# One step list for a whole attention and gated-MLP kernel in place of two, with new tables of PSUM banks and 2 KB buffers

## The chip, the cores and the metric

The kernel runs on one core of a Trainium2 chip. The time is that of the whole launch on the device, in microseconds (us); the figure for the kernel before is the median of three runs. A profile of one further execution gives, for every instruction, when it started, how long it took and which semaphore ended the wait before it. Engine names are those of the profile: PE (TensorE, matmuls), PEld (its weight loads), DVE (VectorE), ACT (ScalarE), POOL (GpSimd) and SP (SyncE, which issues every DMA here).

## What is computed

The reference, cut to what matters:

```
q, k, v: (8 batches, 8 heads, 576 tokens, 64)
k_p, v_p = mean of k, v over groups of 8 tokens            # 72 pooled tokens
attn     = softmax(q @ k_p.T / 8)                          # 576 x 72 a head
x        = (attn @ v_p), heads side by side                # (4608 tokens, 512)
xn       = x / sqrt(mean(x*x) + 1e-6) * rms_g
g, val   = xn @ w_gate, xn @ w_val                         # 512 -> 1536
out      = (silu(g) * val) @ w_out                         # 1536 -> 512
```

## The kernel before, in words

Every large product is made of three matmuls on numbers split into a high and a low part (high by high, low by high, high by low), each 128x128 by 128x512.

- **Attention** goes by batch b (0 to 7) and pair of heads p (0 to 3). The scores of a pair are the step `sc` (20 small matmuls into two PSUM tiles `pss`, line 441); then come maximum, exponential and normalisation on DVE, ACT and POOL. For batches 0 and 1 the probabilities are turned by TensorE (step `ft`, tiles `pst`, line 501). For batches 2 to 7 DVE turns them, they go to HBM and come back (steps `dw` and `dm`, tensors `turn`, `pt`). The product with the pooled v is the step `av`, one for each half u of the tokens (tile `psx`, line 523).
- **The MLP** goes by blocks i of 512 tokens (0 to 8) and chunks f of 128 hidden columns (0 to b, in base 36). Blocks 0 to 2 run 12 matmuls for the gate (`mg`) and 12 for the value (`me`, both line 1027). Blocks 3 and 4, 5 and 6, 7 and 8 run as pairs with seven products of block halves (Strassen's scheme): the steps `pr` (line 829, six matmuls, tiles `px` and `py`). Each `pr` reads its weights from HBM into one of **eight ring buffers** (tile `wp`, step `rl`, line 816): load m can be issued only when the product that used load m-8 is done. The second product is `mo` or its half `mp` (line 1079, tile `po`), and for the last pair `dp` (line 964), whose loads `dr` share the eight buffers.
- **The weights** arrive as float64 in 26 pieces and are taken apart in the first stage by ACT and DVE (steps `ca`, `cb`, `cc`, `cd`, `ch`, `cl`; the last one writes the low part, line 331).

The order of the work is written out: `ORDER` for the first stage, `LATER` for the rest, each a list of step names, and nothing is rescheduled. Every engine runs the steps that are its own in the order of the list, and waits for semaphores. PSUM has eight banks. In `ORDER` the digits behind a colon name the bank of each new PSUM tile, elsewhere the call does (as `BANK1`, `BANK2` and `DBANK`). Small 2 KB buffers have fixed roles: one for `act`, one for `hl`, two for `hh`, two named by the table `OUTS`.

Of the kernel before, what the change touches and what calls it, by code (L numbers as in the profile page):

```python
# [31 lines left out]

# [14 lines left out]

# [44 lines left out]
LATER = """  # L92
lk22 wt0 sc20:01 mg10 mx200 sb200 me10 gt10 mx201 ex200 lk21 lq21 kt1 sm200 mg11 vl10 wf00 wh01 nm200 hi10 lo10 wl01
wf01 ws01 sb201 ex201 me11 pk21 pk22 wf02 gt11 sm201 wd0 nm201 wh02 sc21:01 lk23 lv21 vl11 tr20 hi11 wh03 wl03 mo10
lq22 mx210 sb210 wl02 wf03 dw20 lo11 mx211 ex210 ws02 mg12 ws03 sm210 nm210 pk23 pv21 sb211 me12 ex211 wh04 gt12 sm211
dm20 sc22:01 lk30 nm211 tr21 dw21 wl04 mo11 wt1 mx220 sb220 vl12 ex220 hi12 ws04 lq23 av200:0 mx221 sm220 nm220 lo12
mg13 xc200 wf10 sb221 pk30 ex221 sm221 nm221 wh11 wl11 av201:1 lv22 ws11 gt13 dm21 me13 wf11 tr22 dw22 wf12 xc201 xd20
sq20 wh12 wl12 sc23:01 vl13 wf13 ws12 hi13 mo12 mx230 wh13 lq30 mx231 sb230 ex230 wl13 lo13 ws13 sm230 av210:0 dm22
pv22 nm230 mg14 xc210 wh14 sb231 lk31 wl14 ex231 sm231 wt2 av211:1 xd21 gt14 me14 lv23 nm231 wf20 pk31 xc211 sq21 jn21
av220:0 vl14 wd1 ws14 hi14 wh21 wl21 ws21 av221:1 mo13 xc220 pv23 xd22 tr23 xc221 lv30 dw23 wf21 wh23 lo14 mg15 wl23  # L100
sq22 ws23 jn22 sc30:01 pv30 lk32 gt15 me15 mx300 lq31 mx301 dm23 vl15 sb300 wf22 wh22 ex300 wl22 mo14 wf23 wh24 ws22
hi15 lo15 sm300 nm300 sb301 wl24 wt3 mg16 wd2 ws24 pk32 av230:0 me16 xc230 ex301 gt16 wf30 wh31 wl31 wf31 av231:1
xc231 xd23 sq23 jn23 lv31 wd3 ws31 mg17 mo15 vl16 hi16 sm301 lo16 sh2 wf32 wh32 wl32 gt17 ws32 sl2 rm21:1 rm20:0 rt20
wh33 nm301 tr30 wf33 wd4 pv31 dw30 me17 rc20 wl33 rt21 rc21 wh34 wl34 sc31:01 lq32 ws33 lk33 wt4 mo16 dm30 ws34 rs20
mg18 wf40 vl17 rs21 wh41 hi17 me18 wl41 ws41 wf41 mx310 sb310 ex310 lo17 wf42 mx311 wd5 gt18 sm310 av300:0 pk33 mo17
nm310 sb311 wh42 wh43 wl42 ws42 vl18 xc300 hi18 wl43 lo18 ws43 av301:1 lv32 xd30 ex311 mg19 sm311 nm311 tr31 xc301
sq30 wf43 wh44 wd6 wl44 sc32:01 mx320 lq33 ws44 gt19 me19 sb320 dw31 lk40 mx321 ex320 sm320 wt5 wf50 nm320 wh51 mg1a
mo18 vl19 hi19 sb321 ex321 lo19 wl51 ws51 wf51 sm321 wh53 pv32 wl53 nm321 tr32 wf52 wh52 sc33:01 mx330 pk40 dm31 dw32
me1a gt1a vl1a mx331 sb330 wl52 ex330 lq40 lk41 dm32 ws53 ws52 mo19 sm330 hi1a lo1a av310:0 mg1b nm330 sb331 ex331
xc310 sm331 nm331 wf53 pk41 av311:1 tr33 gt1b me1b lv33 xd31 dw33 xh20 xh21 xh22 xl21 xl20 av320:0 xh23 xl23 xl22 mo1a  # L110
xc311 xc320 kt2 wh54 wl54 wt6 wd7 vl1b hi1b pv33 lo1b ws54 sc40:01 dm33 mx400 lq41 sq31 jn31 sb400 mx401 ex400 mo1b
ev11 wf60 lk42 st11 mg20 sm400 nm400 ev10 sb401 ex401 sm401 st10 av321:1 gt20 nm401 av330:0 xd32 lv40 me20 xc321 pk42
xc330 ev12 sq32 jn32 st12 av331:1 xc331 wh61 vl20 mg21 wd8 hi20 wl61 ws61 xd33 lo20 wf61 lv41 pv40 sq33 jn33 ev13 st13
tr40 me21 gt21 wf62 sh3 dw40 sl3 rm30:0 rt30 vl21 rm31:1 mo20 hi21 rt31 lo21 wh63 wh62 wl62 wf63 ws62 sc41:01 lk43
mg22 mx410 lq42 sb410 wl63 ws63 pv41 mx411 ex410 dm40 wh64 me22 sm410 nm410 gt22 pk43 wl64 sb411 ex411 wt7 rc31 ws64
sc42:01 lk50 vl22 mo21 wf70 sm411 hi22 lo22 nm411 lq43 wd9 wh71 wl71 tr41 mg23 wf71 ws71 mx420 sb420 dw41 wf72 wh73
wl73 mx421 ex420 sm420 ws73 av400:0 me23 xc400 gt23 nm420 sb421 rs31 wh72 ex421 av401:1 xd40 wl72 wf73 vl23 hi23 mo22
lv42 sm421 dm41 xc401 ws72 lo23 wh74 nm421 rc30 sc43:01 mx431 wl74 ws74 wt8 mg24 lq50 mx430 pv42 wf80 tr42 dw42 me24
gt24 rs30 sb430 ex430 av410:0 mo23 dm42 wda vl24 sq40 sm430 hi24 xc410 yh30 lo24 nm430 mg25 yh31 yl30 wh81 sb431 yl31
ex431 av411:1 wl81 ws81 wf81 gt25 sm431 me25 wf82 lv43 pk50 nm431 wh82 xd41 xc411 sq41 jn41 av420:0 xc420 vl25 wdb  # L120
av421:1 hi25 mo24 tr43 lk51 xc421 wh83 wl83 wl82 ws82 lo25 dw43 wf83 xd42 pv43 mg26 ws83 sq42 jn42 lv50 me26 pk51 gt26
wh84 wl84 ws84 wt9 mo25 vl26 dm43 hi26 lo26 wf90 pv50 mg27 wh91 wl91 wf91 ws91 wf92 gt27 wh93 av430:0 wl93 av431:1
lv51 xc430 ws93 me27 xc431 xd43 sq43 wh92 jn43 mo26 wl92 ws92 sh4 vl27 sl4 rm41:1 wf93 hi27 wh94 lo27 wl94 pv51 rm40:0
ws94 mg28 rt40 rt41 rc40 me28 gt28 rs40 rc41 wta wfa0 wha1 wla1 mo27 wfa1 wsa1 wfa2 wha3 vl28 rs41 hi28 wla3 yh32 mg29
wsa3 lo28 wha2 wla2 ys33 me29 gt29 wsa2 yh33 wfa3 wha4 wla4 wtb mo28 ys34 yh34 wsa4 yl33 vl29 hi29 lo29 yl34 ys36 ys35
wfb0 whb1 wlb1 wfb1 yl32 wsb1 me2a mg2a gt2a whb3 yh35 wfb2 whb2 mo29 yh36 vl2a hi2a wlb2 wfb3 wsb2 wlb3 wsb3 lo2a
yl35 mg2b gt2b yl36 whb4 wlb4 me2b rl300 mo2a rl301 wsb4 vl2b hi2b lo2b mo2b rl302 rl303 rl304 rl305 ev20 st20 ev21
st21 pr300 cp30 pr301 u230 pr302 rl306 rl310 sa30 ev23 st23 kt4 ev22 st22 pr303 u330 pr304 c230 rl311 pr305 rl312 sw30
rl313 pr310 v230 rl314 vb30 pr306 v130 cp31 rl315 sc50:01 lk52 va30 pr311 rl316 lq51 hi30 mx501 lo30 pr312 u231 rl320
mx500 sb500 sa31 pk52 ex500 rl321 rl322 pr313 rl323 pr314 u331 rl324 pr315 c231 v231 rl325 sw31 mp300 mp301 rl326 vb31  # L130
# [102 lines left out]
def body(ctx: ExitStack, tc: tile.TileContext, qT, kT, vN, w1, w2, gain, out):  # L233
# [959 lines left out]
```

## Time and profile before

| | |
|---|---|
| median of 3 runs | 981.77 us (981.32 to 983.97) |
| profiled execution, first to last instruction (span) | 980.6 us |
| outside the span (median less span) | 1.2 us |
| PE busy | 963.3 us, 98% |
| DVE, ACT, POOL busy | 695.5, 488.6, 291.6 us |
| moved by DMA | 189.39 MB, mean 193 GB/s |

Busy time is the union of an engine's instructions. The ends of matmuls are modelled, so a busy PE need not be PE at its peak: what a stretch costs is better read from the starts.

### The profile page before, as it was taken

How to read it: one execution, taken by the hardware profiler on the slowest of the kernel's cores; microseconds unless marked ns; L12 is line 12 of the kernel's file. 1: busy time of each engine (PE TensorE's matmuls, PEld its weight loads, DVE VectorE, ACT ScalarE, POOL GpSimd, SP SyncE). 2: the span in 40 equal slices, each digit the busy share in tenths (PEclk: the TensorE clock that was granted, in tenths of full speed). 3: DMA queues.
4: the chain of work that ended last, by engine and by line, in shares of the span. 5: the costliest groups of instructions: out<-in, count | busy, mean ns of one | idle time of the engine just before them, and what ended most of it. 6: DMA issues, size and time to landing. Idle time of an engine off the chain costs nothing.

```text
span 980.6 us, 14131 instructions
## 1 busy us (share of the span) xinstructions
PE 963.3 (98%) x4784; PEld 758.1 (77%) x4784; DVE 695.5 (71%) x1139; ACT 488.6 (50%) x904; POOL 291.6 (30%) x285
## 2 busy tenths in 40 slices
PE   8999989999999999999999999999999999999998
PEld 7677768777777778787777778777888787888886
DVE  7999986866777858557777788876544745545565
ACT  6975765654665644347465554764223422223232
POOL 2200121666646576101111022355341001113230
PEclk9999999999999999999999999999999999999999
DMA  9436512787788751758786661877676506666665
GB/s 313 163 141 242 205 36 72 217 248 241 242 234 245 206 167 54 255 180 232 215 234 195 202 180 53 261 226 223 201 226 214 203 32 214 194 192 193 195 191 185
DMA packets 130199, 189.39 MB, mean 193 GB/s; under 512 B 10896, under 2 KB 76944, under 8 KB 128848
## 3 DMA queue, kind: packets, MB, share of 16 engines
q1 hardware_dynamic: 130128, 188.49, 62.6%
q8 instruction: 38, 0.62, 0.3%
q14 instruction: 33, 0.27, 0.1%
HBM read 132.22 MB, written 56.23 MB: 192 GB/s over the span
## 4 chain that ended last, share of the span: by engine, by line
PE 82%; DVE 6%; ACT 4%; DMA 3%; issue 2%; POOL 1%; SPq 1%; DVEq 0%; ACTq 0%; POOLq 0%
PE po L1079 20%; PE py L829 18%; PE psg L1027 17%; PE px L829 14%; PE pd L964 6%; PE pss L441 3%; PE psx L523 3%; DMA wp<-blocks 1%; DVE hl L1065 1%; ACT main L419 1%; POOL wt L751 1%; DMA turn<-sq 1%; DMA wx<-w 1%; DVE wt L313 1%; DVE mx L407 1%
## 5 line engine op out<-in xcount | busy, mean ns | idle before, releaser
L829 PE MATMUL py<-xp,wp 128*128 128x512 f32 x864 | 221.6, 392 | 1.4 <-DVE u L1149 0.8
L829 PEld LDWEIGHTS py<-xp,wp 128*128 128x128 f32 x864 | 160.8, 188 | 39.6 <-DVE u L1150 1.7
L1027 PE MATMUL psg<-xh,w 128*128 128x512 f32 x576 | 183.3, 400 | 2.1 <-DVE w L331 1.2
L1079 PE MATMUL po<-w,hh 128*128 128x512 f32 x672 | 174.3, 390 | 0.0
L829 PE MATMUL px<-xp,wp 128*128 128x512 f32 x648 | 166.9, 393 | 0.4 <-DMA wp<-blocks 0.3
L1079 PEld LDWEIGHTS po<-w,hh 128*128 128x128 f32 x672 | 126.1, 188 | 27.1 <-issue 0.4
L829 PEld LDWEIGHTS px<-xp,wp 128*128 128x128 f32 x648 | 120.1, 188 | 30.9 <-issue 2.7
L1027 PEld LDWEIGHTS psg<-xh,w 128*128 128x128 f32 x576 | 106.0, 189 | 33.7 <-issue 7.0
L1027 PE MATMUL psg<-xl,w 128*128 128x512 f32 x288 | 112.8, 393 | 0.0
L472 POOL TENSOR_TENSOR prob<-prob,sm 128x360 f32<-128x360 f32 x48 | 42.2, 880 | 228.1 <-DVE sm L468 164.1
L1079 PE MATMUL po<-w,hl 128*128 128x512 f32 x336 | 97.5, 399 | 1.6 <-DVE hl L1065 1.5
L1079 PEld LDWEIGHTS po<-w,hl 128*128 128x128 f32 x336 | 61.2, 188 | 20.0 <-DVE hl L1065 3.8
L1065 DVE TENSOR_TENSOR hl<-act,hh 128x512 fp32r<-128x512 f32 x60 | 50.0, 833 | 23.7 <-ACT hh L1057 20.2
L1143 ACT COPY hb<-px 128x512 f32<-128x512 f32 x36 | 21.1, 587 | 87.1 <-PE px L829 87.1
L1027 PEld LDWEIGHTS psg<-xl,w 128*128 128x128 f32 x288 | 54.4, 189 | 12.2 <-DVE xl L1016 0.4
L1148 ACT ACTIVATE hb<-hb 128x512 f32<-128x512 f32 x36 | 22.7, 632 | 80.8 <-DVE hb L1147 80.7
L1146 DVE TENSOR_TENSOR u<-u,py 128x512 f32<-128x512 f32 x36 | 24.6, 684 | 52.6 <-PE py L829 52.6
L964 PE MATMUL pd<-dp,wq 128*128 128x512 f32 x252 | 61.0, 389 | 0.0
L1057 ACT CAST hh<-act 128x512 fp32r<-128x512 f32 x60 | 37.2, 619 | 46.6 <-DVE act L1151 25.4
L964 PEld LDWEIGHTS pd<-dp,wq 128*128 128x128 f32 x252 | 47.3, 188 | 9.9
L751 POOL TENSOR_TENSOR wt<-wsum,wt 128x256 fp32r<-128x256 f32 x48 | 41.3, 865 | 38.6 <-ACT wt L747 38.5
L1150 DVE TENSOR_TENSOR u<-u,py 128x512 f32<-128x512 f32 x36 | 24.6, 683 | 32.5 <-PE py L829 32.4
(165 smaller groups left out, 1506.7 us busy)
## 6 DMA issues: line engine op xcount, KB each, us to landing
wp<-sum SPq DMA_DIRECT2D x144, 256.0 KB
wp<-blocks SPq DMA_DIRECT2D x108, 256.0 KB
sum<-wt SPq DMA_DIRECT2D x48, 256.0 KB
blocks<-w SPq DMA_DIRECT2D x24, 512.0 KB
wx<-w SPq DMA_DIRECT2D x10, 1024.0 KB
v<-vN SPq DMA_DIRECT2D x32, 288.0 KB
wx<-w SPq DMA_DIRECT2D x16, 512.0 KB
k<-kT SPq DMA_DIRECT2D x28, 288.0 KB
```

The lines of the kernel that those rows point to most:

```text
L441: nc.tensor.matmul(s["ps", h][:, t * SP:(t + 1) * SP], s["q"][r, o:o + P], s["pk"][r, :], start=True, stop=True)
L472: nc.gpsimd.tensor_tensor(l_pr(h), l_pr(h), sm[:, :, None].broadcast_to([P, len(OFFS2), SP]), ALU.mult)
L523: nc.tensor.matmul(ps[r, :n], s["pv"][:, r], x, start=True, stop=True)
L751: nc.gpsimd.tensor_sub(y[:, 1], place(f, f"T{k}"), y[:, 0].bitcast(F32))
L829: nc.tensor.matmul(ps[:, :NB], w[:, a, c, :], x[:, b, c, :], start=j == 0 and not more, stop=j == len(todo) - 1, skip_group_check=more)
L964: nc.tensor.matmul(ps[:, :NB], w[:, a, c * P:(c + 1) * P], x[b], start=g == 0 and j == 0 and not more, stop=g == HF - 1 and j == 2, skip_g ...
L1027: nc.tensor.matmul(ps[:, :NB], w[:, c, cols], x[c], start=(j == 0), stop=(j == len(todo) - 1))
L1057: nc.scalar.copy(a, act_in(i, f))
L1065: eng.tensor_sub(l, act_in(i, f), hh[i, f].bitcast(F32))
L1079: nc.tensor.matmul(po[i, t], x[i, f][:, t * P:(t + 1) * P], w, start=(f == 0 and k == 0), stop=(f == NF - 1 and k == 2))
L1146: u3=lambda i, f: V.tensor_add(u3(i), u2(i), st["Y", i, f, 3]),
L1150: v1=lambda i, f: V.tensor_add(u2(i), u2(i), st["Y", i, f, 5]),
```

## The change

Every step of the two lists stands once in the new list `PLAN`, with the same arguments, on the same engine; the warm-up matmuls are as many (48) in groups of the same sizes. What is new is the order, and where tiles lie: each new PSUM tile takes its bank from the table `BANKS`, and six 2 KB buffers named `cell0` to `cell5` serve `act`, `hl`, `hh`, the outputs and the small weight tiles alike, each taken in turn from the table `CELLS`. The table of the four staging buffers (`STAGES`) has new numbers too. The diff, cut to its core (of each table a line):

```
-ORDER = """
-zg:0 k01 q00 k00 v00 K01 q01 v01 q02 k02 v03 v02 k03 q03 l3 l1 K00 S00:01 V00 M000 E000 M001 l0 z1:7 S01:45 M010 M011
...
-OUTS = """
-0101001100111001101001010101010101010101010010101100101010101010101011001010100110101010101010101010101010011010
...
-DBANK = {5: dict(A=(2, 3), B=(4, 5), C=(6, 7), D=(2, 3)), 7: dict(A=(6, 7), B=(0, 1), C=(2, 3), D=(4, 5))}
...
+PLAN = """
+zzg lk00 lq00 pk00 sc00 lk01 pk01 lq01 fm000 fe000 fm001 sc01 fm011 fm010 lv00 pv00 fe011 lk02 pk02 fr000 zza fe001
...
+CELLS = """
+1220431524023502421530213543252305123512430142504135412310543510301523410412320515404153043202435045143205213405243501
...
+BANKS = """
+7601536724154676471032572340514730630041724560307172104372156050160551605015060105601056051605106105607641230471523632
...
+    stages, cells, banks = ([x for x in y if x.isdigit()] for y in (STAGES, CELLS, BANKS))
...
+    def cell(shape, dt, name):
+        return sb1.tile(shape, dt, tag=f"cell{cells.pop(0)}", name=name)
+
+    def bank(name):
+        return psum.tile([P, 512], F32, tag=f"bank{banks.pop(0)}", name=name)
...
-        t = st["act", i, f] = sb1.tile([P, NB], F32, tag="act", name=f"act{i}_{f}")
+        t = st["act", i, f] = cell([P, NB], F32, f"act{i}_{f}")
...
-            l = sb1.tile([P, NB], F32R, tag="act" if second(i) and f % 2 else "hl", name=f"hl{i}_{f}")
+            l = cell([P, NB], F32R, f"hl{i}_{f}")
...
+    def run():
+        for step in PLAN.split():
+            STEPS[step[:2]](*(int(x, 36) for x in step[2:]))
+        assert not (stages or cells or banks)
```

How instructions moved is shown at three places. Lines have other numbers in the changed kernel: 331 became 327, 523 became 513, 829 became 819, 816 became 806.

**DVE, first stage, the low part of the gate and value weights of chunk 9** (`w1_9`, from the piece `wt18`; `wt20` to `wt23` are later pieces, `mx1_3` the maxima of batch 1, pair 3, `psg0_8` the products of block 0, chunk 8). Before:

```order
L313 SCALAR_TENSOR_TENSOR wt18_1182<-wx9_1178,wt18_1182 128x1024
L545 COPY xraw1_650<-psx1_2_1_1234 128x288
L305 TENSOR_SCALAR wt22_1274<-wt22_1274 128x512
L1038 TENSOR_TENSOR act0_8_1277<-xraw0_322,psg0_8_0_1237 128x512
L309 SCALAR_TENSOR_TENSOR wt22_1274<-wx22_1189,wt22_1274 128x512
L305 TENSOR_SCALAR wt20_1282<-wt20_1282 128x1024
L305 TENSOR_SCALAR wt23_1280<-wt23_1280 128x512
L309 SCALAR_TENSOR_TENSOR wt20_1282<-wx10_1191,wt20_1282 128x1024
L309 SCALAR_TENSOR_TENSOR wt23_1280<-wx23_1250,wt23_1280 128x512
L407 TENSOR_REDUCE mx1_3_1304<-pss1_3_0_1292 128x5
L408 TENSOR_SCALAR mx1_3_1304<-mx1_3_1304 128x5
L407 TENSOR_REDUCE mx1_3_1304<-pss1_3_1_1293 128x5
```

Two rows on stands `L331 TENSOR_TENSOR w1_9`. In the changed kernel:

```order
L309 SCALAR_TENSOR_TENSOR wt18_1227<-wx9_1222,wt18_1227 128x1024
L535 COPY xraw1_638<-psx1_2_1_1239 128x288
L1051 TENSOR_TENSOR hl0_7_1252<-act0_7_1183,hh0_7_1249 128x512
L1024 TENSOR_TENSOR act0_8_1254<-xraw0_355,psg0_8_0_1209 128x512
L397 TENSOR_REDUCE mx1_3_1271<-pss1_3_1_1257 128x5
L398 TENSOR_SCALAR mx1_3_1271<-mx1_3_1271 128x5
L301 TENSOR_SCALAR wt20_1244<-wt20_1244 128x1024
L327 TENSOR_TENSOR w1_9_1289<-wt18_1227,w1_9_1289 128x1024
```

Between the finished piece and its low part stood twelve instructions; now there are six.

**PE, blocks 5 and 6, the two `av` steps of batch 7, pair 1** (`psx7_1_0` and `psx7_1_1`). Before:

```order
L829 MATMUL py5_2_3_6228<-xp5_5_5848,wp5_2_3_6164 128x512 x6
L523 MATMUL psx7_1_0_6244<-pt7_1_6168,pv7_1_5644 64x256 x2
L829 MATMUL px5_2_4_6249<-xp5_2_5814,wp5_2_4_6166 128x512 x6
L829 MATMUL py5_2_5_6266<-xp5_3_5817,wp5_2_5_6186 128x512 x6
L1079 MATMUL po5_1_6053<-w2_1_657,hh5_1_6184 128x512 x2
L1079 MATMUL po5_2_6055<-w2_1_657,hh5_1_6184 128x512 x2
L1079 MATMUL po5_3_6057<-w2_1_657,hh5_1_6184 128x512 x2
L523 MATMUL psx7_1_1_6295<-pt7_1_6168,pv7_1_5644 64x320 x2
L829 MATMUL py5_2_5_6266<-xp5_6_5888,wp5_2_6_6197 128x512 x6
```

In the changed kernel:

```order
L819 MATMUL py5_2_3_6234<-xp5_5_5906,wp5_2_3_6175 128x512 x6
L513 MATMUL psx7_1_1_6243<-pt7_1_6241,pv7_1_5641 64x320 x2
L513 MATMUL psx7_1_0_6255<-pt7_1_6241,pv7_1_5641 64x256 x2
L819 MATMUL px5_2_4_6264<-xp5_2_5844,wp5_2_4_6248 128x512 x6
L819 MATMUL py5_2_5_6280<-xp5_3_5849,wp5_2_5_6195 128x512 x6
L819 MATMUL px5_3_0_6295<-xp5_0_5401,wp5_3_0_6293 128x512 x6
```

The two halves stand next to each other, so full-size matmuls are interrupted once and not twice.

**PE and SP, blocks 3 and 4, the weights of product 6 of chunk 1** (`wp3_1_6`). Before, PE ran the products of a chunk in the order 0 to 6 and SP issued the loads in the same order. In the changed kernel PE has:

```order
L819 MATMUL px3_1_4_4092<-xp3_2_3929,wp3_1_4_3997 128x512 x6
L819 MATMUL px3_2_0_4106<-xp3_0_3536,wp3_2_0_4104 128x512 x6
L819 MATMUL py3_1_5_4116<-xp3_3_3758,wp3_1_5_4114 128x512 x6
L819 MATMUL py3_2_1_4126<-xp3_4_3763,wp3_2_1_4051 128x512 x6
L819 MATMUL py3_1_5_4116<-xp3_6_3969,wp3_1_6_4133 128x512 x6
```

and SP:

```order
L806 DMA wp3_1_4_3997<-sum1_4_2144 128x512
L806 DMA wp3_0_2_3999<-blocks0_1576 128x2x256
L1089 DMA out<-o2_0_3964 128x512
L745 DMA sum9_4_4031<-wt9_4_3884 128x512
L806 DMA wp3_1_1_4035<-sum1_2_2013 128x512
L806 DMA wp3_0_6_4047<-blocks0_1576 128x2x256
...
L806 DMA wp3_1_3_4082<-sum1_3_1997 128x512
...
L806 DMA wp3_2_0_4104<-blocks2_2665 128x2x256
L806 DMA wp3_1_5_4114<-sum1_1_1967 128x512
L745 DMA sum11_4_4123<-wt11_4_4029 128x512
L806 DMA wp3_1_6_4133<-blocks1_2254 128x2x256
```

The load of `wp3_1_6` takes the ring buffer of `wp3_1_4`, eight loads back, and three products stand between the product that frees this buffer and the one that needs the load. Before, the same load took a buffer that was freed at least seven groups of six matmuls earlier.

## Rows read from the trace of the kernel before

**Rows 1.** The page: span, then busy us (share) and instructions of each engine.

```profile
span 980.6 us, 14131 instructions
...
PE 963.3 (98%) x4784; PEld 758.1 (77%) x4784; DVE 695.5 (71%) x1139; ACT 488.6 (50%) x904; POOL 291.6 (30%) x285
```

**Rows 2.** Waits of PE: us in total, times, longest us.

```profile
PE pst L501 <- POOL prob L431: 2.0, 2, 1.3
...
PE px L829 <- DMA wp<-blocks: 0.3, 1, 0.3
```

**Rows 3.** Windows of 25 us: busy time (instructions) by engine, granted clock, DMA share, GB/s.

```profile
100.00:125.00 25.00, 24.57 (x128) 18.74 (x127) 24.78 (x40) 18.10 (x41) 2.65 (x2) 1.00 0.54 192
125.00:150.00 25.00, 22.25 (x96) 16.73 (x95) 21.14 (x36) 15.79 (x40) 7.55 (x6) 0.93 0.13 36
...
475.00:500.00 25.00, 25.00 (x129) 19.05 (x126) 18.36 (x35) 14.17 (x23) 7.07 (x6) 1.00 0.76 213
...
850.00:875.00 25.00, 25.00 (x112) 20.69 (x111) 12.58 (x19) 5.92 (x10) 2.59 (x2) 1.00 0.65 192
```

**Rows 4.** Timeline of PE, block 1: start us, length us, operation.

```profile
190.67 0.65 PE L523 MATMUL psx<-pt,pv 72*64 72x256 f32 x4
191.25 0.73 PE L1027 MATMUL psg<-xh,w 128*128 128x512 f32 x2
...
194.21 0.76 PE L523 MATMUL psx<-pt,pv 72*64 72x320 f32 x4
...
197.84 1.34 PE L441 MATMUL pss<-pk,q 64*128 64x72 f32 x20
...
209.23 1.19 PE L523 MATMUL psx<-pt,pv 72*64 72x256 f32 x8
210.35 1.21 PE L1079 MATMUL po<-w,hl 128*128 128x512 f32 x4
...
213.25 0.61 PE L1027 MATMUL psg<-xh,w 128*128 128x512 f32 x2
```

**Rows 5.** The chain that ended last: a group of 12 matmuls between groups.

```profile
213.41 2.72 PE psg L1027 x12
```

**Rows 6.** Timeline of PE, first stage; in brackets the idle time before and its releaser.

```profile
119.92 1.20 PE L1079 MATMUL po<-w,hl 128*128 128x512 f32 x4 [0.43 <-DVE hl L1065]
...
128.04 0.50 PE L1027 MATMUL psg<-xh,w 128*128 128x512 f32 x1 [0.68 <-DVE w L331]
...
132.12 0.63 PE L501 MATMUL pst<-ident,prob 128*72 128x128 f32 x4 [1.29 <-POOL prob L431]
133.53 0.91 PE L1027 MATMUL psg<-xh,w 128*128 128x512 f32 x2 [0.78 <-DVE act L1047]
...
137.98 1.08 PE L1079 MATMUL po<-w,hl 128*128 128x512 f32 x4
```

**Rows 7.** Timeline of DVE: the finished piece 18 and its low part.

```profile
119.78 1.22 DVE L313 SCALAR_TENSOR_TENSOR wt<-wx,wt 128x1024 uint32<-128x1024 uint32 x1
...
126.77 1.22 DVE L331 TENSOR_TENSOR w<-wt,w 128x1024 fp32r<-128x1024 f32 x1
```

**Rows 8.** Timeline of PE, later stages: idle time before and its releaser.

```profile
398.41 0.50 PE L1079 MATMUL po<-w,hl 128*128 128x512 f32 x1 [0.86 <-DVE hl L1065]
...
682.79 1.42 PE L829 MATMUL py<-xp,wp 128*128 128x512 f32 x5 [0.55 <-DVE u L1150]
...
813.10 1.65 PE L829 MATMUL py<-xp,wp 128*128 128x512 f32 x6 [0.78 <-DVE u L1149]
```

**Rows 9.** The costliest group of ACT table loads: busy us, mean ns of one, idle before.

```profile
L462 ACT ACT_TABLE_LOAD x36 | 46.2, 1283 | 0.7
```

**Rows 10.** The chain again: DMAs on it, from issue to landing.

```profile
573.06 4.49 DMA pt<-turn
645.77 3.60 DMA turn<-sq
650.29 6.24 DMA wp<-blocks
```

More of the change, by code (lines that the diff above doesn't have):

```diff
@@ L335, in body @@
     st = {}
-    given = []
-    def bank(k, name):
-        return psum.tile([P, 512], F32, tag=f"bank{given.pop(0) if given else k}", name=name)
     def main(p):
@@ L493, in s_pt, with s_ptcopy @@
         s = st[b, p]
+        ps = s["pst", h] = bank(f"pst{b}_{p}_{h}")
+        for j, (k, t) in enumerate([(h, t) for t in range(4)] if h < 2 else [(0, 4), (1, 4)]):
+            nc.tensor.transpose(ps[:SP, j * P:(j + 1) * P], s["pr", k][:, t, :], ident)
+    def s_ptcopy(b, p, h, copy):
+        s = st[b, p]
         if "pt" not in s:
@@ L498, in s_pt @@
                 s["pt"] = stage([SP, 2, S], F32, f"pt{b}_{p}")
-        ps = s["pst", h] = bank(0, f"pst{b}_{p}_{h}")
-        for j, (k, t) in enumerate([(h, t) for t in range(4)] if h < 2 else [(0, 4), (1, 4)]):
-            nc.tensor.transpose(ps[:SP, j * P:(j + 1) * P], s["pr", k][:, t, :], ident)
-    def s_ptcopy(b, p, h, copy):
-        s = st[b, p]
         ps = s["pst", h]
@@ L513, in s_av @@
         s = st[b, p]
-        ps = s["psx", u] = bank(0, f"psx{b}_{p}_{u}")
+        ps = s["psx", u] = bank(f"psx{b}_{p}_{u}")
         n = S // 2 if b in EARLY else (256, S - 256)[u]
@@ L590, in l_total @@
     def l_total(b, u):
-        ps = st["rms", b, u] = bank(0, f"psr{b}_{u}")
+        ps = st["rms", b, u] = bank(f"psr{b}_{u}")
         for k in (0, 1):
@@ L953, in d_bank @@
         if key not in st:
-            st[key] = bank(DBANK[i][m][c], f"pd{i}_{n}_{c}")
+            st[key] = bank(f"pd{i}_{n}_{c}")
         return st[key]
@@ L967, in d_keep @@
     def d_keep(i, n, c):
-        if n == 0:
-            t = sb2.tile([P, NB], F32, tag="hh", name=f"m1_{i}_{c}")
-        else:
-            t = sb1.tile([P, NB], F32, tag=("hl", "act")[c], name=f"m4_{i}_{c}")
-        st["m", i, n, c] = t
+        t = st["m", i, n, c] = cell([P, NB], F32, f"m{n}_{i}_{c}")
         nc.scalar.copy(t, d_bank(i, n, c))
@@ L1018, in mm1 @@
     def mm1(i, f, which):
-        ps = st["psg", i, f, which] = bank(2 + which, f"psg{i}_{f}_{which}")
+        ps = st["psg", i, f, which] = bank(f"psg{i}_{f}_{which}")
         cols = slice(which * P, (which + 1) * P)
@@ L1090, in o_copy @@
         else:
-            o = spare([P, DM], F32, name)
+            o = cell([P, DM], F32, name)
         st["o", i, t] = o
```

416 lines of the change are left out of this document (199 added, 217 removed).

## The prediction

> **What bounds the kernel now.** I read the page first: PE is busy 98% of the span, no other engine over 71% [rows 1]. The work is the same in both kernels, so the change can win only idle time of PE or time that PE spends inside its busy share on something else than matmuls. Idle time is 980.6 - 963.3 = 17.3 us in all. The waits of PE put only a part of it down to named causes, none over 2 us in total, and 0.3 us to a weight load of the ring [rows 2].
>
> The windows show two regimes. Around 100 to 125 us DVE is busy 24.78 of 25 us, beside a PE at 24.57: the weights are taken apart just in time, and DVE sets the pace. From 475 us on PE fills its windows and DVE has slack (18.36 and 12.58 of 25) [rows 3]. So the first stage has to be argued from DVE's queue, the rest from PE's own order and from what is late for it.
>
> The timeline shows what a busy PE hides. Between groups of 12 full matmuls, a group takes 2.72 us from start to start [rows 5]. In block 1 a lone first half of an `av` begins at 190.67 and the next interruption at 194.21: 3.54 us, of which 2.72 are the group, so 0.82 go to the interruption. The second half costs 197.84 - 194.21 - 2.72 = 0.91. Where both halves stand together, 209.23 to 213.25 less 2.72 leaves 1.30; this distance leaves out one entrance from full matmuls, which is the 2.96 of the group between two interruptions (191.25 to 194.21) less the 2.90 of the one followed by a full group (210.35 to 213.25), 0.06. So 1.73 apart against about 1.36 together [rows 4]; I take **0.35 us for each pair of halves put together**.
>
> **The change, part by part.** *Fewer interruptions.* Counted in the order from block 1 on, full matmuls are interrupted 46 times, before 68. Of the halves of `av`, 24 follow another `av` directly, before 9: 15 x 0.35 = 5.25 us off PE's path, with nothing that could hide it, since PE is the bound there [rows 3, 4]. Six times a half stands next to an `sc`, before never. The trace of this part shows no such neighbours. Between 0 (each keeps both switches) and 0.35 (as two halves) I take the middle, 0.17: 1.0 us. Bounds of this part: 5.25 and 7.4; **taken: -6.3**.
>
> *First stage.* PE stands idle here at five places that the new order treats: before 119.92 (0.43, for the low part of a hidden chunk), 128.04 (0.68, for DVE's low part of the weights of chunk 9), 132.12 (1.29, for normalised probabilities of batch 1, pair 3) and 133.53 (0.78). Then 12 matmuls take 137.98 - 133.53 = 4.45 us in place of 2.72, while the granted clock of this window falls to 0.93: the lower of the two levels (1.2 of 2.4 GHz) for most of that group, after PE had been idle twice. Together 0.43 + 0.68 + 1.29 + 0.78 + 1.73 = 4.9 us [rows 3, 6]. In the new order four groups of 12 instead of two stand between the scores of that pair and its transposes (10.9 against 5.4 us at 2.72 each), the low part for 119.92 has an `av` and an `sc` before it as cover, and on DVE the low part of chunk 9 comes after six instructions instead of twelve: before, 126.77 - 119.78 - 1.22 = 5.8 us passed between [rows 7]; half of that is some 3 us earlier. DVE is the pace here, and what was moved behind this row must still be done: first of all later pieces of the output weights (those of chunks 7 to 9), which PE also needs later now. Bounds: nothing, if DVE merely pushes its lateness on (window 125 to 150 has 3.9 us of DVE idle to take it up [rows 3]), and 4.9. PE's order has the cover, so **taken: -4.9**.
>
> *Buffers.* 398.41 waits 0.86 for the low part of a hidden chunk that could not be written while the matmuls before still read the only `hl`; with six cells it is written earlier. 813.10 (0.78) has its bank freed by DVE right before the next product; in the new order three other products stand between. 682.79 (0.55) waits behind a reciprocal on DVE that is moved [rows 8]. **Taken: -2.2**; the many shorter waits stay as they are. Against this stand new tight places: the first ring load of block 3 has one group of 2.72 as cover since the last user of its buffer, one `sc` follows a group that has to be read out of its bank first, and one `pr` of block 5 takes a bank that ACT has just read. None has a row; between 0 and the largest such wait now, 0.86 each [rows 8], I take 0.5: **+1.5**.
>
> *The ring.* This is what the new order gives away. Products and loads no longer go round in step, so the time between the end of the product that frees a buffer and the start of the one that needs the next load shrinks. Counted in groups of 1.36 us (half of 2.72): before, no load of a `pr` had less than seven groups, 9.5 us. Now 12 loads of 286 have under 5 us (most of them three groups, 4.08), 13 more have four groups (5.44). In this time SP must issue and the load land. The page gives no landing time. The chain has three DMAs: 120 KB in 3.60, 324 KB in 4.49, and a 256 KB ring load in 6.24, issued behind a transfer that SP had waited for [rows 10]. By size 256 KB lies at 4.2: 12 x 0.11 = 1.3 us, and I add one load as late as the row, 6.24 - 4.08 = 2.2. **Taken: +3.5**, bounds 0 (at 3.60) and 12 x 2.2 + 13 x 0.8 = 37 (all at 6.24). SP's queue belongs here: seven fetches of turned probabilities (`dm`) stand directly behind the store that they wait for, before three, so SP stands still for up to 3.60 us with ring loads behind it. The Trainium skill, DMA: Bandwidth & Descriptors, Anatomy of one DMA, fits a DMA of the GpSimd path with 2.0 us and 1 us for each 436 KB, so 256 KB would land in 2.6 us (an estimate from that page), and this term would be nothing and the sum 3.5 us lower; the rows of this case, from SP's queue, are all longer.
>
> *At nothing:* 75 table loads on ACT in place of 92, 17 x 1.28 = 22 us [rows 9], since ACT is busy 50% of the span and PE's waits do not name it among the long ones [rows 1, 2]; should ACT be late somewhere, this helps. The start (scores of pair 0 first, other order of loads) has the same 48 warm-up matmuls and one more `sc` before the first gate product, while a wait of PE there goes away: nothing, within 1.5 us.
>
> Sum: -6.3 - 4.9 - 2.2 + 1.5 + 3.5 = -8.4. The profiled span of 980.6 becomes 972.2, and with the 1.2 us between it and the median of the runs **973.4 us**.
>
> **Rivals.** *Late ring loads make it slower.* One mechanism: a product waits because its buffer was freed three or four groups ago. For it: the 6.24 [rows 10], and DMA share 0.76 at blocks 3 and 4; against it: 0.65 from 850 us on, where eight of the twelve tightest loads lie [rows 3]. Without the ring term the sum is -11.9. It decides when 12 x (L - 4.08) passes 11.9, that is, at a mean time from release to landing L of 5.07 us. At 5.5 it is 17.8 us, and the kernel takes 973.4 - 3.5 + 17.8 = 987.7. Chance 0.13. The rule of the same page, Rules for kernel authors, speaks on this side: issue a DMA early and wait for it late; the wait of 0.3 us in all under the old, wide cover agrees [rows 2].
>
> *DVE passes its lateness on.* DVE is as full as before, the first stage ends when it did, and 4.9 us stay: 978.3. For it: 24.78 of 25 us [rows 3]; against it: PE's stalls there came from order, not only from DVE's sum [rows 6]. Chance 0.2.
>
> *The ring costs nothing:* loads land in under 4.1 us as the smaller ones on the chain do [rows 10]: 973.4 - 3.5 = 969.9. Chance 0.2.
>
> **How the numbers follow.** The forecast has 0.47, the rivals 0.13, 0.2 and 0.2. Low end: no ring term, no new waits, neighbours at the full price: 973.4 - 3.5 - 1.5 - 1.1 = 967, and 2 us for short waits that go too: 965. High end: the second rival with the ring at 10 us is 984.8, rounded to 985; of the slower rival about half lies beyond. A measurement of this kernel can tell about 0.3%, 2.9 us, from no change. Faster by more (under 978.8): the forecast, the cheap ring and half of the second rival, 0.77, less something for what I have not seen: 0.75. Within: 0.13. Slower: 0.12.
>
> **What would show it.** In the new profile: `psx` rows of eight matmuls in place of four; no group of 12 at 4.45 us and no granted clock under 1.00 after 50 us; the first matmul of block 1 some 5 us earlier; no wait of 0.8 us before the last chunk of block 2. Late ring loads would show as PE `px` and `py` waiting for DMA `wp` with microseconds in place of 0.3. The prediction is wrong if these waits pass 10 us, or if DVE is still busy 24.8 of 25 us up to the end of block 0 and that end lies where it was.

## The result, and where the time went

The changed kernel takes **975.52 us** (median of 5 runs, 969.70 to 977.08) against 982.82 us before (5 runs, 981.32 to 983.97). The ratio is 0.9908, with a 95% interval of 0.9884 to 0.9932: faster by some 9 us by the ratio, by 7.3 between the medians. The forecast was 973.4. The profiled execution is one of the shorter ones: 969.70 us, with a span of 967.9.

The page of the changed kernel, to be set beside [rows 1] (span; busy us, share and instructions by engine; granted TensorE clock in 40 equal slices, in tenths):

```profile
span 967.9 us, 13903 instructions
...
PE 956.3 (99%) x4784; PEld 767.3 (79%) x4784; DVE 681.9 (70%) x1139; ACT 460.9 (48%) x887; POOL 287.4 (30%) x285
...
PEclk9699999999999999999999999999999999999999
```

Idle time of PE fell from 17.3 to 967.9 - 956.3 = 11.6 us, which is less than half of the 12.7 us that the span lost. The second slice (24 to 48 us) reads 6: the clock fell there, as it had not before. The windows of the changed kernel (25 us each, columns as in [rows 3]) say the same:

```profile
25.00:50.00 25.00, 22.86 (x144) 18.08 (x145) 17.39 (x36) 17.55 (x50) 8.46 (x6) 0.66 0.44 151
...
100.00:125.00 25.00, 25.00 (x131) 20.25 (x129) 24.86 (x42) 18.41 (x41) 2.33 (x2) 1.00 0.40 146
125.00:150.00 25.00, 25.00 (x125) 19.52 (x122) 22.24 (x38) 16.56 (x41) 6.46 (x5) 1.00 0.24 76
...
475.00:500.00 25.00, 25.00 (x128) 19.51 (x129) 19.09 (x35) 15.89 (x23) 4.37 (x4) 1.00 0.76 230
...
850.00:875.00 25.00, 25.00 (x112) 20.69 (x111) 12.52 (x18) 5.65 (x10) 2.58 (x2) 1.00 0.62 196
```

From 100 to 150 us PE now fills its windows, where [rows 3] had 24.57 and 22.25, and DVE is as full as it was up to 125 us. The waits of PE (total us, times, longest) name other things than [rows 2]:

```profile
PE pst L486 <- POOL main L421: 2.6, 3, 1.6
...
PE pss L431 <- ACT main L409: 1.0, 1, 1.0
PE psx L513 <- ACT own L499: 0.8, 1, 0.8
...
PE psg L1013 <- ACT act L1020: 0.6, 1, 0.6
...
PE po L1065 <- DVE hl L1051: 0.2, 1, 0.2
```

All but the last two of these lie in the first 30 us. No wait for ring weights (tile `wp`) is left in the list of this execution.

For an account that adds up, I counted the distances between the starts of successive matmuls over both traces. A full matmul followed by another takes 0.2267 us; what is above that is a wait or a slow clock; what lies between two full ones across small matmuls is an interruption. The first stage ends where the first full matmul of block 1 starts, in the kernel before and in the changed one:

```profile
165.70 0.73 PE L1027 MATMUL psg<-xh,w 128*128 128x512 f32 x2
```

```profile
165.26 0.62 PE L1013 MATMUL psg<-xh,w 128*128 128x512 f32 x2
```

The table goes by the rows of the timelines. (Behind the table, as in the expectations, the first gate product is given by its own start, which is 0.24 us ahead of its row.)

| profiled executions, us | before | after | change |
|---|---|---|---|
| first gate product starts | 41.2 | 50.6 | +9.5, of which 1.5 is an `sc` now done earlier: **+8.0** |
| from there to block 1: interruptions, waits and low clock | 26.6 | 16.7, with that `sc` (1.5) gone from here | -9.9, without the `sc` **-8.4** |
| from block 1 on: interruptions with nothing late | 73.9 | 67.5 | **-6.5** |
| from block 1 on: waits, inside interruptions and out | 10.9 | 5.0 | **-5.8** |
| sum (the last matmul starts at 976.6 and 963.9) | | | -12.7 |

The forecast had 0, -4.9, -6.3 and +2.8 (-2.2 + 1.5 + 3.5) in these places. Its sum of -8.4 lies between this profile and the medians (-7.3), and errors on both sides hide in it: a loss at the start that it didn't have, and first-stage and later waits that went further than it said.

**The start.** The timeline of PE in the changed kernel (start, length, operation, in brackets the idle time before and its releaser), and two rows of block 1 to which we come back:

```profile
25.26 0.63 PE L486 MATMUL pst<-ident,main 128*72 128x128 f32 x4 [0.78 <-POOL main L421]
...
29.32 1.28 PE L486 MATMUL pst<-ident,main 128*72 128x128 f32 x5 [1.61 <-POOL main L421]
...
33.62 2.41 PE L431 MATMUL pss<-pk,q 64*128 64x72 f32 x20
...
50.64 1.62 PE L1013 MATMUL psg<-xh,w 128*128 128x512 f32 x6
...
192.81 1.19 PE L513 MATMUL psx<-pt,pv 72*64 72x256 f32 x8
...
196.92 1.34 PE L431 MATMUL pss<-pk,q 64*128 64x72 f32 x20
```

PE waits twice for POOL, and the scores that follow at 33.62 take 2.41 us, where the same 20 matmuls take 1.34 later. The granted clock in windows of 5 us is 0.75 from 25 us, 0.50 from 30 and from 35, 0.54 from 40, and 1.00 from 45 on: the lower of the two levels (1.2 of 2.4 GHz) for some 17 us. POOL is late because two of its instructions take 2.27 and 3.67 us:

```profile
22.93 2.27 POOL L421 TENSOR_TENSOR main<-main,mx 128x360 f32<-128x360 f32 x1 [0.77 <-DVE mx L416]
25.60 3.67 POOL L421 TENSOR_TENSOR main<-main,mx 128x360 f32<-128x360 f32 x1 [0.39 <-DVE mx L416]
```

The same two in the kernel before:

```profile
23.41 0.80 POOL L431 TENSOR_TENSOR main<-main,mx 128x360 f32<-128x360 f32 x1 [1.84 <-DVE mx L426]
25.14 1.07 POOL L431 TENSOR_TENSOR main<-main,mx 128x360 f32<-128x360 f32 x1 [0.93 <-DVE mx L426]
```

And what DVE does beside the longer one, in the changed kernel:

```profile
25.94 1.28 DVE L305 SCALAR_TENSOR_TENSOR wt<-wx,wt 128x512 uint32<-128x512 uint32 x2
...
27.34 1.28 DVE L309 SCALAR_TENSOR_TENSOR wt<-wx,wt 128x512 uint32<-128x512 uint32 x2
```

Four instructions with two inputs in SBUF stand nearly back to back there, 2.56 us in all; before, they were spread among others. POOL's instruction ends 3.67 - 0.79 = 2.88 us late. The Trainium skill, SBUF — State Buffer, Who interferes with whom, states that an instruction of VectorE with two inputs in SBUF contends with one of GpSimd that reads SBUF, over a pair of ports that one of them holds alone, and that the order of issue decides which of the two is blocked. The trace agrees on the first: POOL's delay of 2.88 us is about as long as the four instructions of DVE. It doesn't show the second plainly: POOL's row begins at 25.60, ahead of DVE's 25.94 (where a POOL instruction starts is only roughly known), and POOL is late by four instructions, not by one.

### The profile page after: what moved, and what is told of

Read it like the earlier page. It is cut to its first block, busy times and chain, and to the rows that moved or that the text cites. A ratio compares the mean times of both kernels' runs of the same rounds, so it can differ in the third digit from the quotient of the medians.

```text
span 967.9 us, 13903 instructions
## 1 busy us (share of the span) xinstructions
PE 956.3 (99%) x4784; PEld 767.3 (79%) x4784; DVE 681.9 (70%) x1139; ACT 460.9 (48%) x887; POOL 287.4 (30%) x285
## 4 chain that ended last, share of the span: by engine, by line
PE 93%; DVE 3%; DMA 1%; ACT 1%; POOL 1%; issue 1%; SPq 0%; POOLq 0%; ACTq 0%
PE po L1065 23%; PE psg L1013 20%; PE py L819 19%; PE px L819 15%; PE pd L954 6%; PE pss L431 4%; PE psx L513 3%; PE warm L1095 1%; PE pst L486 1%; DMA mix<-mixed 1%; DMA sum<-wt 0%; DVE own L388 0%; PE psr L606 0%; POOL main L421 0%; DVE mx L397 0%
## 5 line engine op out<-in xcount | busy, mean ns | idle before, releaser
L819 PE MATMUL py<-xp,wp 128*128 128x512 f32 x864 | 215.2, 391 | 0.2
L1013 PE MATMUL psg<-xh,w 128*128 128x512 f32 x576 | 180.2, 395 | 0.6 <-ACT act L1020 0.6
L819 PE MATMUL px<-xp,wp 128*128 128x512 f32 x648 | 162.8, 391 | 0.0
L1013 PEld LDWEIGHTS psg<-xl,w 128*128 128x128 f32 x288 | 54.1, 188 | 11.6
L1122 DVE TENSOR_TENSOR u<-u,py 128x512 f32<-128x512 f32 x36 | 24.7, 685 | 53.0 <-PE py L819 52.9
L741 POOL TENSOR_TENSOR wt<-wsum,wt 128x256 fp32r<-128x256 f32 x48 | 37.8, 796 | 75.7 <-ACT wt L737 75.5
L1051 DVE TENSOR_TENSOR hl<-act,hh 128x512 fp32r<-128x512 f32 x60 | 45.5, 759 | 17.5 <-ACT hh L1043 11.0
L566 POOL TENSOR_TENSOR acc<-acc,sq 128x576 f32<-128x576 f32 x21 | 30.9, 1470 | 58.9 <-ACT sq L557 58.6
```

The lines of the kernel that those rows point to most:

```text
L566: nc.gpsimd.tensor_add(acc[b], acc[b], st[b, p]["sq"])
L741: nc.gpsimd.tensor_sub(y[:, 1], place(f, f"T{k}"), y[:, 0].bitcast(F32))
L819: nc.tensor.matmul(ps[:, :NB], w[:, a, c, :], x[:, b, c, :], start=j == 0 and not more, stop=j == len(todo) - 1, skip_group_check=more)
L1013: nc.tensor.matmul(ps[:, :NB], w[:, c, cols], x[c], start=(j == 0), stop=(j == len(todo) - 1))
L1051: eng.tensor_sub(l, act_in(i, f), hh[i, f].bitcast(F32))
L1122: v1=lambda i, f: V.tensor_add(u2(i), u2(i), st["Y", i, f, 5]),
```

## The experiments

**The start: the kernel once more.** No edit.

> The changed kernel once more, nothing edited. Its five times fell into two groups, 970 and 976 to 977 us, with mean granted clocks of 0.991 to 0.993 and 0.988 to 0.989. Theory A (the start): PE waits for late POOL results at 20 to 29 us, the clock falls to the lower level, and how long it stays there decides the group. Then a profile of the longer kind shows the low clock for some 23 us in place of 17, all of it before 55 us, and the stretch from the first gate product to the end as long as in the first profile (913.7 us from 50.4 to 964.0). Rival B: the two groups differ later, in late ring loads; then PE shows waits for the ring's weights and the first gate product starts at 50.4 in both kinds.

Measured: 971.54 us (970.76 to 973.04), ratio 0.9885 (0.9869 to 0.9900). POOL's two instructions take 2.27 and 3.67 us again, the clock falls in the same place, and the first gate product starts at 49.0. The longer kind of execution didn't come, so its profile is not here. In the nine timed executions of the changed kernel a lower mean clock goes with a longer time: 969.7 to 971.6 at 0.991 to 0.993, 973.0 at 0.990, 975.5 to 977.1 at 0.986 to 0.989. That the clock of the start makes the longer ones longer is likely from this, and not shown: none of them was profiled.

**The start: DVE's instructions out of POOL's way.** The global list, cut to the steps that move:

```
-... ld2 cb1 fa021 ldb ft020 cb0 av000 ... fa010 cc1 ya000 ... fa022 cc0 fn031 ... fv012 cd1 cd0 fz20
+... ld2 fa021 ldb ft020 av000 ... fa010 ya000 ... fa022 fn031 ... fv012 cb1 cb0 cc1 cc0 cd1 cd0 fz20
```

> The changed kernel with six steps of DVE (cb1, cb0, cc1, cc0, cd1, cd0, the taking apart of pieces 0 and 1) moved behind the copy fv012, so that POOL's two normalisations fn030 and fn031 no longer meet them. Nothing else moves. Theory A: these DVE instructions held POOL up (2.27 and 3.67 us in place of 0.79), PE waited 0.78 and 1.61 us for it and then ran at the lower clock from 27.5 to 44 us. Then fn030 and fn031 take about 0.8 us each, the granted clock stays at 1.00, the first gate product starts at 42 to 44 us in place of 50.4, and the kernel takes 7 to 9 us less than the shorter group, 961 to 963 us. Rival B: DVE is the pace of the first stage, so that an earlier first gate product is paid back by waits before block 1: the first gate product is early, but the first matmul of block 1 lies within 2 us of 174.7, and the time stays at 968 to 970. Rival C: the order itself makes the start late; then the first gate product stays at 49 us or later.

Measured: **965.02 us** (963.65 to 967.42), ratio 0.9819 (0.9801 to 0.9837), and 6.5 us less than the changed kernel beside it, a little short of the 7 to 9 expected. POOL's timeline and two windows of 5 us of this run:

```profile
24.09 0.79 POOL L410 TENSOR_TENSOR main<-main,mx 128x360 f32<-128x360 f32 x1 [2.35 <-DVE mx L405]
25.88 0.85 POOL L410 TENSOR_TENSOR main<-main,mx 128x360 f32<-128x360 f32 x1 [1.00 <-ACT own L486]
```

```profile
25.00:30.00 5.00, 4.16 (x28) 2.14 (x28) 4.67 (x13) 4.79 (x14) 1.80 (x2) 1.00 0.89 299
30.00:35.00 5.00, 4.53 (x45) 3.70 (x44) 4.39 (x11) 4.97 (x18) 2.73 (x2) 1.00 0.89 270
```

The same two instructions take 0.79 and 0.85 us, the clock stays up, and the first gate product starts at 43.5. The first matmul of block 1 starts at 158.9 in place of 165.3, so DVE doesn't take the gain back:

```profile
158.93 0.62 PE L1002 MATMUL psg<-xh,w 128*128 128x512 f32 x2
```

The expectations name 174.7 and 168.3 for it. That is the gate product of chunk 0 of block 1, which in the new order stands 36 full matmuls and an `sc`, some 9.5 us, behind the first matmul of the block; the difference is the same. Theory A holds; B and C fall.

**The same once more,** for the question whether the start can still lose its clock:

> The changed kernel with DVE's six steps moved once more, nothing else, beside the other runs on the same chip. If the clock of the start was what set the time, every execution shows a mean granted clock of 0.998 or more and the times lie at 963 to 968 us, with the first gate product at 42 to 44 us. If the first run was luck (the start can still lose its clock), some executions show 0.991 or less and take 971 us or more.

Measured: 965.33 us (964.84 to 973.71, 6 runs), ratio 0.9839 (0.9812 to 0.9865). Five executions lie at 964.8 to 967.7 with clocks of 0.996 to 1.000; one shows 0.992 and takes 973.71. In the profiled one the first gate product starts at 41.8 and block 1 at 157.2. So the cause is right, and the cure is not complete.

**The start: the clock alone.** Warm-up matmuls where PE waits, with POOL as late as it was:

```
-... fz00 ft022 ft030 ... av021 ft032 ft031
+... fz00 ft022 zz6 ft030 ... av021 zzg ft032 ft031
```

> The changed kernel with 22 more warm-up matmuls where PE waits for POOL: 6 ahead of the step ft030 and 16 ahead of ft032 (0.7 and 1.8 us at the higher clock). POOL stays late. This tells the clock apart from the lateness. Theory A1: most of the loss is the clock; it stays at 1.00, the first gate product starts at 43 to 45 us and the kernel takes 6 to 8 us less than the shorter group. Theory A2: most of it is the lateness of the results; then the first gate product stays at 48 us or later, whatever the clock shows.

Measured: 972.38 us (971.99 to 972.86), ratio 0.9892 (0.9878 to 0.9905), no gain over the changed kernel beside it. PE and POOL in this run:

```profile
29.29 3.84 PE L1084 MATMUL warm<-ident 128*128 128x128 f32 x32
33.19 0.85 PE L475 MATMUL pst<-ident,main 128*72 128x128 f32 x6
...
48.58 2.08 PE L1002 MATMUL psg<-xh,w 128*128 128x512 f32 x8
```

```profile
26.86 3.67 POOL L410 TENSOR_TENSOR main<-main,mx 128x360 f32<-128x360 f32 x1 [0.39 <-DVE mx L405]
```

I had mis-priced my own edit: 16 warm-up matmuls take 3.84 us and not 1.8, and hold PE until 33.1, 2.6 us after POOL was done. So the time, which agrees with A2, decides nothing. The stretch behind it does: with the clock at 1.00 it is 48.58 - 33.19 = 15.4 us from these transposes to the first gate product, and 16.0 in both profiles with DVE's steps moved, against 50.64 - 29.32 = 21.3 in the changed kernel. The low clock costs 5.3 to 5.9 us, and POOL's lateness (0.78 + 1.61) most of the rest of the 8.0.

**The start: two more waits.** On top of DVE's moved steps:

```
-... fm030 ld0 ca0 fv001 ... ld1 ca1 fr010 ... av001 lv01 ft021 pv01 lv02 fm031 ... fa010 ya000
+... fm030 lv01 lv02 ld0 fv001 ... ld1 fr010 ... av001 ft021 pv01 fm031 ... fa010 ca0 ca1 ya000
```

> The run with DVE's six steps moved (965.0 us), and two more moves in the first 25 us: the loads of the v tiles of pairs 1 and 2 are issued ahead of the first two weight pieces, which fill the DMA engines there, and ACT takes these pieces (ca0, ca1) after the copies of the probabilities and not ahead of them. Theory: the v tile landed late (DVE waited 1.45 us for it in that profile) and ACT stood on a piece not yet landed, with the copy that PE waited 1.07 us for behind it. Then both waits go, the first gate product starts at 41.5 to 42.5 us in place of 43.5, no execution shows a mean granted clock under 0.998, and the time is 961 to 963.5 us. Rival: DVE is the pace of the first stage, so the earlier start is given back before block 1 starts (168.3 us): 964 to 966 us.

Measured: 969.61 us (964.06 to 973.36, 6 runs), ratio 0.9859 (0.9831 to 0.9887). Worse: the theory falls. PE's wait for ACT's copy at 20 us went from 1.07 to 0.35, and others came in its place, as this row and this window show:

```profile
26.76 1.23 PE L502 MATMUL psx<-own 72*64 72x288 f32 x4 [1.03 <-ACT own L488]
```

```profile
25.00:30.00 5.00, 3.95 (x18) 1.86 (x20) 4.00 (x9) 4.14 (x10) 1.53 (x2) 0.65 0.88 287
```

The clock falls at about the same place. It does so in three of its six executions (0.990 and 0.991, 971.8 to 973.4 us) and not in the other three (0.999 and 1.000, 964.1 to 967.4). That is the plainest measure of the clock here: the same program, some 7 us apart.

**Fifteen pairs of halves taken apart.** On the changed kernel, as in this place of block 1 and in fourteen more (the banks follow their tiles):

```
-... av200 ... av201 ... me13
+... av200 ... me13 av201
```

> The changed kernel with 15 of the pairs of av halves of blocks 1 to 6 taken apart again: the second half is moved behind the next product on PE. Work, banks and buffers stay. Theory: an interruption shared by two halves saves 0.35 us, so this costs 15 x 0.35 = 5.2 us, in the trace as lone halves of 0.78 and 0.89 us in place of 1.33 for both. Rival: the gain from block 1 on came from fewer short waits and not from the pairing; then it costs under 2 us. A cost of over 8 us would mean that new waits for banks came with it.

Measured: 992.98 us (990.22 to 993.71), ratio 1.0095 (1.0077 to 1.0113): 21 us more than the changed kernel, and not 5. Part of it is the start (first gate product at 52.9 in the profile, with unchanged code). From block 1 on the profile is 19.0 and 21.5 us longer than the two of the changed kernel. Fourteen more interruptions are 5.1 of it, as expected; the waits are the rest, 21.4 us against 5.0 and 7.5. Seven of the fifteen places cost 0.348 us each and nothing else; in the others something is late, as here, where the matmul behind the second half waits for a bank:

```profile
329.99 0.65 PE L502 MATMUL psx<-pt,pv 72*64 72x256 f32 x4
332.09 0.74 PE L1002 MATMUL psg<-xh,w 128*128 128x512 f32 x2 [1.45 <-DVE xraw L520]
```

Behind three of these waits the clock falls too: the granted clock is 0.93 in the windows of 25 us from 200, 325 and 650 us, where it is 1.00 in the changed kernel. Three times 0.07 of 25 us, some 5 us of the 21.4, is this and not waiting.

**The seven clean pairs alone,** on the run with DVE's moved steps, same edit:

> The run with DVE's six steps moved (965.0 us), with seven pairs of av halves taken apart: those seven of the fifteen whose separation cost nothing but the interruption in the trace of the run that split them all. Theory: 7 x 0.348 = 2.4 us more, 967.4; in the trace seven lone halves more of each kind, 0.784 and 0.890 us. Rival: the price of a pair taken apart is mostly the waits that come with another order, as in that run (17 to 21 us for fifteen); then it is 6 us or more.

Measured: 970.51 us (969.50 to 970.82), ratio 0.9874 (0.9860 to 0.9888): 5.5 us more than the 965.02 of that run, between the two. The trace has seven lone halves more of each kind, at 0.78 to 0.80 and 0.89 to 0.96: 2.4 us, as priced. Waits of 2.9 come at four pairs that were not edited and take 1.5, 1.8, 2.4 and 2.6 us in place of 1.33, but others go: from block 1 on all waits sum to 8.4 us, and to 9.1 and 8.3 in the two profiles without the edit. So this stretch is 1.7 and 2.5 us longer, which is the price of the seven pairs. Of the rest, 1.3 us lie between the first gate product and block 1, where nothing was edited. The price is right, and the 5.5 us between the medians are not all the edit's: a pair moved by one product is seldom all that moves.

**Pairs put together in the kernel before.** One part of the change alone, as here and in ten more places:

```
-... av200:0 mx221 sm220 nm220 lo12 mg13 xc200 wf10 sb221 ... av201:1
+... av200:0 av201:1 mx221 sm220 nm220 lo12 mg13 xc200 wf10 sb221 ...
```

> The kernel before with one part of the change alone: in 11 of the 15 places of blocks 1 to 6 where the halves of an av stand apart, the second half is moved up behind the first (in the other four the order allows it only with further moves). Banks, buffers and all other steps stay. Theory: an interruption shared saves 0.348 us, so 11 x 0.348 = 3.8 us less than before, a ratio of 0.996; in the trace 11 pairs more at 1.326 us. Rival: the moved half waits for its bank, or what stands behind it waits, and the gain is lost: within 1 us of before.

Measured: **1004.75 us** (1003.06 to 1009.56), ratio 1.0232 (1.0208 to 1.0255). The rival holds, and more: 22 us lost. The waits of PE, and one of them in the timeline:

```profile
PE psx L509 <- DVE prob L444: 13.5, 8, 3.1
```

```profile
208.43 0.76 PE L509 MATMUL psx<-pt,pv 72*64 72x320 f32 x4 [1.38 <-DVE prob L444]
```

From block 1 on this run is 19.9 us longer than the kernel before; the other 2.5 us of the profile lie ahead of the first gate product, where nothing was edited. Its interruptions cost 3.5 less, near the 3.8 expected, and its waits 23.4 more (34.2 against 10.9). Some 5 us of these are the clock again: 0.86 and 0.93 in the two windows of 25 us from 450, where it was 1.00 before. The second halves of the kernel before go to bank 1, in which the scores of a later pair stand until DVE has read them (`sb221` in the lines above, now behind the `av`). In this order the pairs don't pay without other banks to put them in, which is what the table `BANKS` gives them.

**The ring: loads in the order in which buffers come free.** On the run with DVE's moved steps, 119 loads move up past other loads, as

```
-rl316 ... rl322 ... rl323 ...
+rl322 ... rl323 ... rl316 ...
```

> The run with DVE's six steps moved (965.0 us), and 119 of the 294 ring loads are issued earlier, in the order in which their buffers come free, past other loads only; each load keeps its buffer. In that run PE waited five times for ring weights, 2.0 us in all, and none of the loads that it waited for was one of the eleven whose buffer is freed just three groups (4.08 us) before the use: these took 2.6 to 3.3 us from issue to landing, at once behind the release. The late ones had been issued 4.6 to 8.6 us after their buffer came free, behind a load at the head of SP's queue that waited for its own buffer. Theory: the queue makes them late; then PE's waits for ring weights fall under 0.5 us in all and the time is 963 to 964. Rival: the transfers themselves are slow there (4.3 to 5.6 us from issue to landing); then the waits stay at 1 to 2 us.

Measured: 970.08 us (968.77 to 971.40), ratio 0.9869 (0.9855 to 0.9882), 5 us more. PE's waits for ring weights are 4.2 us in place of 2.0 and 1.5 in the two profiles without the edit:

```profile
PE py L809 <- DMA wp<-sum: 3.8, 3, 3.1
...
PE px L809 <- DMA wp<-blocks: 0.4, 1, 0.4
```

The theory falls as a rule for all loads: a load moved up puts others back, and I can't say from the traces which of them cost how much. Nor do these waits account for all of the 5 us between the medians: the profiled executions, 968.8 us against 967.4 and 964.9, lie closer together.

**Both together.**

> Both of the last two changes together, on top of the run with DVE's six steps moved. If the two theories hold, their gains lie in different stages and add: 959 to 962 us. If one falls, this run is worth no more than the other alone.

Measured: 979.61 us (972.14 to 988.10, 12 runs), ratio 0.9964 (0.9936 to 0.9992). With both theories fallen there is nothing to add up, and this run is worse than either alone. The profile has the low clock of the one (first gate product at 53.0) and the ring waits of the other (6.6 us).

**The ring: one load.** On the run with DVE's moved steps, `rl360` goes ahead of `dw53`, the store of turned probabilities:

```
-... rl356 hi42 pr356 dw53 v135 rl360 pr360
+... rl356 hi42 pr356 rl360 dw53 v135 pr360
```

> The changed kernel with DVE's six steps moved, and one ring load (the first weights of chunk 6 of blocks 3 and 4) issued ahead of the store of turned probabilities that SP waited for; its buffer stays. In all four profiles this load landed just at its use (margin 0.04 to 0.54 us), issued 4.4 to 4.6 us after its buffer came free, because SP stood at that store. Theory: SP's queue makes it late; then it is issued within 0.5 us of the release, lands 3 us or more before its use, and PE's wait of 0.58 us for it goes; the time, 963 to 968, does not tell. Rival: the store or the transfers behind it come later by as much, and PE waits for the probabilities in its place.

Measured: 964.71 us (963.41 to 966.17), ratio 0.9816 (0.9799 to 0.9833); its time doesn't differ from the run without this edit. SP's issues and PE, without the edit (start, length, DMA; the last `wp` is the load in question):

```profile
459.69 0.52 SPq L795 DMA_DIRECT2D wp<-blocks  x1
464.40 2.14 SPq L463 DMA_DIRECT2D turn<-sq  x4
466.65 1.96 SPq L795 DMA_DIRECT2D wp<-blocks  x1
```

```profile
471.01 1.64 PE L808 MATMUL px<-xp,wp 128*128 128x512 f32 x6 [0.58 <-DMA wp<-blocks]
```

and with it (both `wp` loads in the first row):

```profile
459.20 3.03 SPq L795 DMA_DIRECT2D wp<-blocks  x2
463.94 2.80 SPq L463 DMA_DIRECT2D turn<-sq  x4
```

```profile
469.80 1.52 PE L808 MATMUL px<-xp,wp 128*128 128x512 f32 x6
```

The load is issued 0.13 us after its buffer comes free and not 4.6, lands 3.4 us ahead of its use and not 0.04, and PE doesn't wait for it. PE doesn't wait for the probabilities in its place, so the rival falls. For this load the queue was the cause.

## Why the prediction came out, step by step

**Fewer interruptions, -6.3: right in mechanism and size.** Priced by the shortest of each kind, the interruptions from block 1 on cost 73.9 us before and 67.5 now, 6.5 less. The pair at 192.81, a `psx` row of eight matmuls as foretold, shows it: 196.92 - 192.81 - 2.72 = 1.39, near the 1.36 worked out from [rows 4]. The half next to an `sc`, for which no row stood, saves 0.20 (2.05 for an `sc` and a half, 1.47 + 0.78 apart), near the 0.17 taken. What the step left out is its condition: in the kernel before, eleven such pairs made the whole 22 us longer, since their banks weren't free.

**First stage, -4.9: the right places, too small.** The five stalls of [rows 6] are gone, and the granted clock is 1.00 from 50 us on. "PE's order has the cover" is what the runs show: with the first gate product at 41.8 us (DVE's moved steps, second profile), about as early as before for the work done by then, the stretch up to block 1 still has only 17.2 us of interruptions and waits, against 26.6 with one `sc` (1.5) more. So the rival in which DVE passes its lateness on falls, although the first profile looked like it. There the end of block 0 lay where it was, which the prediction had named as a sign of being wrong: the first matmul of block 1 starts at 165.3, against 165.7, and not 5 us earlier. But DVE was no longer full there (22.24 of 25 us in the window from 125), and the 8 us lost at the start hide the gain: with DVE's steps moved the same matmul starts at 158.9 and 157.2. The term measured 8.4. No run took the order of the first stage back by itself, so its cause is read from the rows and not tested. The idle times of rows understate what a stall costs by starts (the transposes with 1.29 and the matmul behind them with 0.78 cost 2.5 in place of 2.1), and there were more stalls than the five that I listed, before 67.81 (0.54 idle, for another low part) and 80.34 (0.60) among them.

**The start, "nothing, within 1.5 us": the step that failed.** It counted PE's steps there, and never set POOL's instructions beside DVE's in the new order. 8.0 us were lost in the profile, and the clock took most of them. With DVE's steps moved, the first gate product starts at 43.5 and 41.8, which for one more `sc` than before (40.9 and 1.5) is 1.1 us late and 0.6 early: without the accident the term would have held. The same clock is the likely reason why the executions of the changed kernel spread over 7 us where those of before lie within 4.

**Buffers -2.2, new tight places +1.5: the three waits of [rows 8] are gone,** and "the many shorter waits stay as they are" was wrong in our favour: outside and inside interruptions they fell from 10.9 to 5.0 us in this profile, to 7.5 in the next. None of the three tight places that I named waited; others did, 0.7 us ahead of the gate product of the last chunk of block 2 (1.0 in the next profile) and 0.4 ahead of a half product `mp` of block 5. So the sign "no wait of 0.8 us before the last chunk of block 2" came out in part: the low part of the hidden chunk no longer stalls PE there, ACT's `act` now does. Which part of the order removed the short waits was not tried.

**The ring, +3.5: mis-sized, and mostly the wrong loads.** The twelve tight loads land 3.1 us after the release of their buffer (median; 3.5 at most in the first profile, under the 4.08 of cover), as the rival with the cheap ring had it. One of them, product 3 of chunk 7 of blocks 3 and 4, is late after all in most other profiles, by 0.1 to 0.8 us. What waits there were (none named in this profile, 0.9 us in the next, 2.0 in the first one with DVE's steps moved) fell mostly on other loads: four of the five of that last run on loads with 9 to 14 us of cover that had stood in SP's queue for 4.6 us and more (the fifth is the tight one), the longest of the next profile (0.68) on one of the loads with four groups of cover, whose transfer took 6.0 us, near the 6.24 of [rows 10]. The working had this queue in one sentence and priced it by the tight loads; the single load moved ahead of a store shows the mechanism, the 119 moved together show that it isn't cured wholesale.

The sum, -8.4, was close by luck: +8.0 left out at the start met 3.5 too little in the first stage and 8.6 too much for waits later. With DVE's six steps moved, the order measures 965.0 and 965.3 us in two runs, ratios of 0.982 and 0.984: that is about what the change without its accident is worth, and no run of this study was clearly faster.

## What to carry to other kernels

When an order is rewritten, set the queues of all engines side by side in the first microseconds, POOL against DVE above all: what the changed order costs may lie in a pair of engines that no dependence joins. A new order and the banks that it needs are one change; the half of it that looks free can cost more than the whole gains. And when a sum comes out, look at each term by itself: here the total came within some 2 us of the median, with most of its terms wrong by more than that.

## What had not been expected of the hardware

A POOL instruction of 0.79 us took 3.67 in each of the four profiles in which four two-input instructions of DVE stood beside it, and 0.79 or 0.85 once these were moved. A few waits of PE among small matmuls, the longest 1.61 us, came with some 17 us at the lower clock (0.50 in the windows from 30 and 35 us), though PE was not idle again behind the last of them; the same program (the run with two more waits mended) went either way from one execution to the next, for 7 us.
